# A gated state-space convolution: the order of the transforms at block ends, and one table load

## The chip, the cores and the metric

The kernel runs on one core of a Trainium2 chip. The core's engines have their own instruction streams: PE (matmuls and their weight loads), DVE (elementwise), ACT (elementwise and activations), POOL (elementwise and DMA issue) and SP (DMA issue). Each works through its stream in order and waits on semaphores for the others. The metric is the time of one execution in microseconds (us). The kernel before takes 539.49 us in the median of three runs (538.57 to 540.05). A profiled execution of it, from which all single times here come, took 540.43 us.

## The reference

For an input `u` of 2048 positions and 512 channels the reference normalizes each position and feeds two branches: a long convolution with a kernel `K` made from a state-space model, plus a skip `u * Dskip`, and a two-layer network with GELU. The result is `u + s * silu(ffn)`.

```python
xn = _layernorm(x, axis=-1)
K  = jnp.einsum("dn,dnl,dn->dl", Cc, P, dB).real      # P = exp(dt*A*l), 2048 long, per channel
Yf = rfft(pad(xn)) * rfft(pad(K))                      # length 4096
s  = irfft(Yf)[..., :L] + xn * Dskip
g  = silu(gelu(xn @ w1 + b1) @ w2 + b2)
out = x + s * g
```

All of it is in float32.

## The kernel before

The first 395 us compute the normalized input, the network and the convolution kernel; matmuls fill PE there. The change does not touch that part. Then the convolution runs in four blocks of 128 channels, b = 0 to 3. A Fourier transform of 2048 positions is split in two stages of matmuls, 64 by 32:

- `first_dft(b, u, h, parts)`, L891, is the first transform. `u` is 0 for the signal and 1 for the kernel, `h` picks 16 of 32 channel columns, and each of the two `parts`, called halves here, fills two PSUM banks. `first_out`, L899, copies them into the big tile `X`, on ACT or, where `engs` says V, on DVE.
- `second_dft(b, g)`, L913, is the second transform, for g = 0 to 7. `spectrum` (L921, ACT) copies the kernel's spectrum `uh` out of PSUM, `product` (L931, DVE) multiplies it with the signal's, and `combine` (L941 and L939, DVE) forms the real and imaginary parts `Y` out of the products of two g.
- `back_dft(b, j)`, L950, is the backward step on one `Y`, with the table `tcn`; `back_out` (L961, ACT) copies it into `Z`. `turn` (L970, DVE) transposes `Z` into `T`.
- `last_dft`, L990, is the last transform, on `T`. It fills four banks `y` at once. `last_out` multiplies them by the gate on DVE (L997) and adds the input on POOL (L998), four of each.

Two g make a slot: blocks 0 to 2 run `two_slots(b, i)` for i = 0 to 3, and in its shadow each slot runs a quarter of the first transform of block b + 1, backward steps of block b or b - 1, and in slot 2 of blocks 1 and 2 the last transform of block b - 1. Block 3 runs `slot(3, g)`, in which nothing is changed. The order of the calls is the order in each engine's stream; no scheduler moves them.

Beside these stand the loads. `side_piece` (L839, SP) fetches a `raw` piece of a later block's signal, four pieces per block; `side_turn` (L858, ACT) reorders it, a quarter at a time, into the first transform's input `in`. `kernel_half` (L874, SP) fetches half of a block's kernel, and `side_skip` (L879, POOL) adds the skip coefficients to that half before `first_dft` with u = 1 reads it. `ct_load` (L817, SP) fetches one of four pieces of the table `tcn`; backward step j of block 0 needs piece j. `tail_load` (L979, SP) fetches gate and input for `last_out`. Each of these is preceded by a one-column DVE memset (`pace`, L801), which sets the time of issue. `loads(b, g, late)` is called twice per g and looks up in a small table which load to issue there.

All banks of L891, L950 and L990 come from one helper, `bank`, which hands out four PSUM banks in turn; the second transform has four banks of its own, two per g.

## Time and profile before

| | |
|---|---|
| median of three runs | 539.49 us (538.57 to 540.05) |
| profiled execution | 540.43 us, span 538.6 us |
| PE busy | 516.0 us (96%) |
| DVE busy | 434.5 us (81%) |
| ACT busy | 388.6 us (72%) |
| POOL busy | 260.5 us (48%) |
| mean granted PE clock | 0.994 of full speed |
| block 0, from its first L913 | 395.25 to 426.95 us |
| block 1 | 426.95 to 459.93 us |
| block 2 | 459.93 to 495.73 us |

The chain that ended last is followed back from the last instruction; each of its rows is a start, a length, and the engine and line that held the end up. A row of a timeline is start, length, engine, line, operation, output and input, the count, and in brackets how long the engine stood idle before it and who released it. Queries by window give busy us and count of PE, the granted clock, the share of DMA time and GB/s.

### The profile page before, as it was taken

Reading aid. Unit: us, or ns where it says so; the run is one execution under the profiler, and the core shown is the slowest. Engines: PE = TensorE matmul, PEld = TensorE weight load, DVE = VectorE, ACT = ScalarE, POOL = GpSimd, SP = SyncE. Lnnn points to the kernel's source line nnn. Section 1 sums busy time; section 2 is a strip of 40 time slices with the busy share of each in tenths; the row PEclk is TensorE's granted clock in tenths of the full one; section 3 lists DMA queues with packets and bytes.
Section 4 is the critical chain, followed back from the end, with each engine's and each line's share of the span. In section 5 each row is a group of like instructions: output and inputs, shape, how many; then the busy total and the mean of one; then the engine's idle time right before and its main releaser. Section 6 shows DMA issues by size and latency. Waiting matters only on the chain.

```text
span 538.6 us, 16527 instructions
## 1 busy us (share of the span) xinstructions
PE 516.0 (96%) x6999; PEld 420.8 (78%) x6999; DVE 434.5 (81%) x732; ACT 388.6 (72%) x552; POOL 260.5 (48%) x384
## 2 busy tenths in 40 slices
PE   8899999999999999999999999999999799898993
PEld 8687788787877777777777777778889798878971
DVE  6998999999998689786875777896377489677896
ACT  3688896999987987896978799797365563633430
POOL 5629376756796576869726464564010004013031
PEclk9999999999999999999999999999999999999997
DMA  8937437843229992354147232952567468242562
GB/s 228 320 103 243 125 128 232 283 146 109 90 80 289 301 277 64 136 151 125 42 130 231 102 80 87 185 138 99 178 231 164 83 218 178 82 160 80 178 204 95
DMA packets 86086, 85.84 MB, mean 159 GB/s; under 512 B 41878, under 2 KB 60698, under 8 KB 84988
## 3 DMA queue, kind: packets, MB, share of 16 engines
q1 hardware_dynamic: 76944, 66.43, 41.9%
q0 software_dynamic: 8768, 17.83, 10.8%
q8 instruction: 55, 0.90, 0.7%
q10 hardware_dynamic: 300, 0.53, 0.3%
q14 instruction: 19, 0.16, 0.1%
HBM read 51.22 MB, written 33.55 MB: 157 GB/s over the span
## 4 chain that ended last, share of the span: by engine, by line
PE 80%; DVE 8%; DMA 3%; ACT 3%; POOL 3%; issue 2%; POOLq 0%; DVEq 0%; ACTq 0%
PE s L913 10%; PE z L287 9%; PE z L289 8%; PE z L288 8%; PE f L248 8%; PE f L250 8%; PE f L249 8%; PE sa L950 5%; PE kg L655 5%; PE s L891 5%; PE ph L591 2%; PE y L990 1%; DMA tcn<-in_ct_dram 1%; DMA w1s<-in_B_w_dram 1%; DVE T L970 1%
## 5 line engine op out<-in xcount | busy, mean ns | idle before, releaser
L616 POOL TENSOR_TENSOR mm<-mm,rc 128x32 f32<-128x32 f32 (+4 forms) x150 | 97.0, 647 | 11.8
L287 PE MATMUL z<-w2h,hh 128*128 128x512 f32 x224 | 95.7, 427 | 0.0
L248 PE MATMUL f<-xh,w1h 128*128 128x512 f32 x220 | 91.6, 416 | 0.2 <-DVE hl L274 0.2
L250 PE MATMUL f<-xh,w1l 128*128 128x512 f32 x220 | 87.0, 396 | 2.5 <-DVE w1l L233 1.5
L289 PE MATMUL z<-w2h,hl 128*128 128x512 f32 x224 | 87.7, 392 | 0.1
L288 PE MATMUL z<-w2l,hh 128*128 128x512 f32 x224 | 87.6, 391 | 0.0
L249 PE MATMUL f<-xl,w1h 128*128 128x512 f32 x220 | 86.8, 395 | 0.0
L913 PE MATMUL s<-X,mc 64*64 64x128 f32 x1536 | 58.3, 272 | 4.7 <-DVE X L899 4.7
L605 DVE SCALAR_TENSOR_TENSOR ra<-ra,ph 128x512 f32<-128x512 f32 x64 | 43.7, 683 | 19.4 <-ACT ra L599 18.5
L931 DVE TENSOR_TENSOR t<-s,uh 128x512 f32<-128x512 f32 x64 | 40.8, 681 | 17.7 <-ACT uh L921 17.3
L921 ACT COPY uh<-s 128x512 f32<-128x512 f32 x32 | 18.8, 586 | 47.9 <-PE s L913 26.3
L913 PEld LDWEIGHTS s<-X,mc 64*64 64x64 f32 x1536 | 45.2, 133 | 9.6 <-DVE X L899 5.3
L262 ACT ACTIVATE f<-f,b1s 128x512 f32<-128x512 f32 x56 | 37.2, 665 | 19.8 <-PE f L250 18.5
L639 DVE TENSOR_TENSOR e<-mm,ra 128x1024 f32<-128x1024 f32 x32 | 43.0, 1347 | 10.3 <-ACT ra L627 4.5
L250 PEld LDWEIGHTS f<-xh,w1l 128*128 128x128 f32 x220 | 41.3, 188 | 12.0 <-DVE w1l L233 2.0
L289 PEld LDWEIGHTS z<-w2h,hl 128*128 128x128 f32 x224 | 42.0, 188 | 10.2 <-DVE hl L274 0.6
L248 PEld LDWEIGHTS f<-xh,w1h 128*128 128x128 f32 x220 | 41.5, 189 | 10.7 <-issue 1.1
L287 PEld LDWEIGHTS z<-w2h,hh 128*128 128x128 f32 x224 | 42.4, 189 | 9.2 <-ACT hh L268 0.4
L613 POOL COPY mm<-rc 128x32 f32<-128x32 f32 x30 | 14.6, 488 | 70.6 <-DVE e L646 39.5
L288 PEld LDWEIGHTS z<-w2l,hh 128*128 128x128 f32 x224 | 42.2, 189 | 8.2
L249 PEld LDWEIGHTS f<-xl,w1h 128*128 128x128 f32 x220 | 41.3, 188 | 9.2
L274 DVE TENSOR_TENSOR hl<-f,hh 128x512 fp32r<-128x512 f32 x56 | 37.7, 681 | 10.8 <-ACT hh L268 10.8
(184 smaller groups left out, 1132.1 us busy)
## 6 DMA issues: line engine op xcount, KB each, us to landing
x<-in_A_u_dram SPq DMA_DIRECT2D x8, 512.0 KB
xs<-x SPq DMA_DIRECT2D x8, 512.0 KB
xt_h<-xh POOLq DMA_DIRECT2D x4, 1024.0 KB, 5.8
xt_l<-xl POOLq DMA_DIRECT2D x4, 1024.0 KB, 8.1
kgd<-ko SPq DMA_DIRECT2D x16, 256.0 KB
za<-zo SPq DMA_DIRECT2D x4, 1024.0 KB
xh<-xt_h POOLq DMA_DIRECT2D x4, 1024.0 KB, 6.6
xl<-xt_l POOLq DMA_DIRECT2D x4, 1024.0 KB, 9.0
```

Source lines behind the costliest of these rows:

```text
L248: PE.matmul(p, wh[:, k, :], xh[:, k, :], start=(k == 0), stop=False)
L249: PE.matmul(p, wh[:, k, :], xl[:, k, :], start=False, stop=False)
L250: PE.matmul(p, wl[:, k, :], xh[:, k, :], start=False, stop=(k == KD - 1))
L274: V.tensor_sub(hl, hf, hh)
L287: PE.matmul(z, hh[:, s], wh, start=(f0 == 0 and not rows), stop=False)
L288: PE.matmul(z, hh[:, s], wl, start=False, stop=False)
L289: PE.matmul(z, hl[:, s], wh, start=False, stop=(f0 == FA - 1))
L605: V.scalar_tensor_tensor(ra[:, 0, c], ra[:, 1, c], MAGIC, p, op0=ALU.subtract, op1=ALU.subtract)
L616: GP.tensor_mul(mv[:, :, 0:3:2, w:2 * w], mv[:, :, 0:3:2, 0:w], rc[:, 2 + 2 * i:4 + 2 * i, :].rearrange("p j c -> p c j").unsqueeze(3).to_ ...
L639: V.tensor_mul(e1, m1.unsqueeze(1).to_broadcast([P, 2, CH, N1]), ra[:, :, :, :N1])
L913: PE.matmul(p[ka * 64:(ka + 1) * 64, r, o, :, jj], w, xf[b][h, c, :, k, :], start=(c == 0), stop=(c == 1), skip_group_check=True)
L931: V.tensor_mul(t, p[:, i, :, 1].unsqueeze(1).to_broadcast([P, 2, 2, P]), uh)
```

## The change

Three things move in `two_slots`, and one in the table of `loads`.

1. At the end of a block (slot 3) both halves of the next block's first transform stand ahead of the backward step, and the combine stands behind it. Before, the second half stood behind the backward step, ahead of the next block's second transform.
2. In slot 2 of blocks 1 and 2 the last transform stands behind both second transforms, which have one half of a first transform between them. The other half goes to slot 3. The multiplications of `last_out` stand behind the combine.
3. The four quarters of `side_turn` stood two at a block's end (slot 3) and two in the next block's slot 0; now one stands in slot 3, ahead of the backward step, two in slot 0 and one in slot 1, behind that slot's first spectrum copy. `turn(b - 1, 1, 1)` goes from the end of slot 1 to the start of slot 2, behind a memset that fetches a raw piece.
4. In block 0 the third piece of `tcn` is loaded at g = 2 instead of g = 4 and the fourth at g = 4 instead of g = 6.

```diff
         if b == 0:
             plan = {(1, 0): lambda: mc_load(2), (1, 1): lambda: ct_load(1), (2, 0): lambda: mc_load(3),
-                    (4, 1): lambda: ct_load(2), (6, 1): lambda: ct_load(3)}
+                    (2, 1): lambda: ct_load(2), (4, 1): lambda: ct_load(3)}
...
+        if end:
+            turn(b - 1, 1, 1)
         second_dft(b, g)
         if end:
-            py = [bank(f"y{b - 1}_{n}").rearrange("p e m -> p (e m)") for n in range(G)]
-            last_dft(b - 1, 0, py)
-            last_dft(b - 1, 1, py)
+            first_dft(*f, (0,))
         second_dft(b, g + 1)
         spectrum(b, g)
-        if b and i == 0:
-            side_turn(b + 1, (2,))
+        if b and i < 2:
+            side_turn(b + 1, (1 + 2 * i,))
         loads(b, g, 0)
         product(b, g)
         if end:
+            first_out(*f, parts=(0,))
+            py = [bank(f"y{b - 1}_{n}").rearrange("p e m -> p (e m)") for n in range(G)]
+            last_dft(b - 1, 0, py)
+            last_dft(b - 1, 1, py)
+            spectrum(b, g + 1)
+            loads(b, g, 1)
+            product(b, g + 1)
+            loads(b, g + 1, 0)
+            combine(b, i, 1)
+            combine(b, i, 0)
             last_out(b - 1, py)
...
+        else:
+            if b and i == 3:
+                k = b + 1, 1, 0
+                first_dft(*k, (1,))
+            first_dft(*f, (0,))
+            spectrum(b, g + 1)
...
+            product(b, g + 1)
+            if b and i == 3:
+                first_out(*k, parts=(1,))
+            if i == 3:
+                first_out(*f, parts=(0,))
+                first_dft(*f, (1,))
+                first_out(*f, (A, A, V, V), (1,))
+                if b + 2 < NB:
+                    side_turn(b + 2, (0,))
+                for k in sa:
+                    back_dft(*k)
+                    back_out(*k)
+                loads(b, g + 1, 0)
+                combine(b, i, 1)
+                combine(b, i, 0)
...
         if b and i == 0:
-            side_turn(b + 1, (3,))
-        if b + 2 < NB and i == 3:
-            side_turn(b + 2, (0, 1))
+            side_turn(b + 1, (2,))
         if b and i < 2:
-            for k in (((0, 0), (0, 1)), ((1, 0), (1, 1)))[i]:
+            for k in (((0, 0), (0, 1)), ((1, 0),))[i]:
                 turn(b - 1, *k)
```

In slots 0 to 2 of block 0 and slots 0 and 1 of the others the calls of the `else` branch keep the order they had.

What this does to the streams is seen best in the order itself. The names: `s1_2_1_0_1_0` is the first transform of block 2, u = 1, h = 0, half 1, its bank 0; `s2_1_4` the second transform of block 1, g = 4; `sa1_1_0` the backward step of block 1, j = 1; `y0_0` the last transform of block 0; numbers behind them are buffer numbers.

PE in block 0, slot 3, before (the first instruction of each call):

```order
L913 MATMUL s2_0_7_5452<-X0_4893,mc_4874 64x2x64 x8
...
L891 MATMUL s1_1_1_1_0_0_5491<-fc_98,in1_1_4980 128x128
...
L950 MATMUL sa0_2_0_5507<-tcn_5040,Y_0_2_5401 128x128
...
L891 MATMUL s1_1_1_1_1_0_5530<-fc_98,in1_1_4980 128x128
...
L913 MATMUL s2_1_0_5548<-X1_5041,mc_4874 64x2x64 x8
```

and now:

```order
L913 MATMUL s2_0_7_5454<-X0_4893,mc_4874 64x2x64 x8
...
L891 MATMUL s1_1_1_1_0_0_5493<-fc_98,in1_1_4980 128x128
...
L891 MATMUL s1_1_1_1_1_0_5509<-fc_98,in1_1_4980 128x128
...
L950 MATMUL sa0_2_0_5523<-tcn_5040,Y_0_2_5403 128x128
...
L913 MATMUL s2_1_0_5547<-X1_5041,mc_4874 64x2x64 x8
```

The half whose copies the next block's second transform needs has gone ahead of the backward step.

PE in slots 2 and 3 of block 1, before:

```order
L913 MATMUL s2_1_4_5824<-X1_5041,mc_4874 64x2x64 x8
...
L990 MATMUL y0_0_5857<-T0_0_5680,gc_5044 32x512
...
L913 MATMUL s2_1_5_5893<-X1_5041,mc_4874 64x2x64 x8
...
L891 MATMUL s1_2_1_0_0_0_5942<-fc_98,in1_2_5753 128x128
...
L891 MATMUL s1_2_1_0_1_0_5965<-fc_98,in1_2_5753 128x128
...
L913 MATMUL s2_1_6_5978<-X1_5041,mc_4874 64x2x64 x8
...
L891 MATMUL s1_2_1_1_0_0_6050<-fc_98,in1_2_5753 128x128
...
L950 MATMUL sa1_1_0_6064<-tcn_5040,Y_1_1_5800 128x128
...
L891 MATMUL s1_2_1_1_1_0_6087<-fc_98,in1_2_5753 128x128
```

and now:

```order
L913 MATMUL s2_1_4_5824<-X1_5041,mc_4874 64x2x64 x8
...
L891 MATMUL s1_2_1_0_0_0_5857<-fc_98,in1_2_5753 128x128
...
L913 MATMUL s2_1_5_5867<-X1_5041,mc_4874 64x2x64 x8
...
L990 MATMUL y0_0_5910<-T0_0_5679,gc_5044 32x512
...
L913 MATMUL s2_1_6_5966<-X1_5041,mc_4874 64x2x64 x8
...
L891 MATMUL s1_2_1_0_1_0_6038<-fc_98,in1_2_5753 128x128
...
L891 MATMUL s1_2_1_1_0_0_6048<-fc_98,in1_2_5753 128x128
...
L891 MATMUL s1_2_1_1_1_0_6066<-fc_98,in1_2_5753 128x128
...
L950 MATMUL sa1_1_0_6080<-tcn_5040,Y_1_1_5800 128x128
```

The last transform went behind the second second transform, one half went to slot 3, and three halves now stand there in a row.

DVE in slots 2 and 3 of block 1, before (the products and multiplications by their first instruction):

```order
L931 TENSOR_TENSOR t0_1_4_5928<-s2_1_4_5824,uh_1_4_5926 128x4x128
...
L997 TENSOR_TENSOR gb0_5045<-y0_0_5857,gb0_5045 128x16x32
...
L931 TENSOR_TENSOR t0_1_4_5928<-s2_1_5_5893,uh_1_5_5952 128x4x128
...
L941 TENSOR_TENSOR Y_1_2_5962<-t0_1_4_5928,t1_1_4_5929 128x2x256
L939 TENSOR_TENSOR Y_1_2_5962<-t0_1_4_5928,t1_1_4_5929 128x2x256
```

and now:

```order
L931 TENSOR_TENSOR t0_1_4_5902<-s2_1_4_5824,uh_1_4_5900 128x4x128
...
L931 TENSOR_TENSOR t0_1_4_5902<-s2_1_5_5867,uh_1_5_5946 128x4x128
...
L941 TENSOR_TENSOR Y_1_2_5954<-t0_1_4_5902,t1_1_4_5903 128x2x256
L939 TENSOR_TENSOR Y_1_2_5954<-t0_1_4_5902,t1_1_4_5903 128x2x256
L997 TENSOR_TENSOR gb0_5045<-y0_0_5910,gb0_5045 128x16x32
```

The multiplications went behind the second product and the combine. POOL's own order is the same in both: four additions L998, then the skip addition L879 for the second kernel half.

## The prediction

> **What bounds the kernel now.** I read the page first, then the chain of work that ended last, then the waits of PE between 380 and 500 us, then each engine's timeline there. The change lies in the slots of blocks 0 to 2, 395 to 496 us of a 538.6 us span; nothing ahead of them is touched.

> ```profile
> PE 516.0 (96%) x6999; PEld 420.8 (78%) x6999; DVE 434.5 (81%) x732; ACT 388.6 (72%) x552; POOL 260.5 (48%) x384
> ```
> ```profile
> PE s L913 <- DVE X L899: 4.7, 3, 1.7
> ```

> PE is busy 96% of the span, so what the change can win is what PE stands idle in its slots. The second fence, of PE's waits, says that 4.7 us of it are three waits of the second transform (L913) for DVE's copies into X (L899): one at each block's end. The chain shows them, and one more loss in block 0:

> ```profile
> 413.94 7.06 DMA tcn<-in_ct_dram
> 421.13 0.68 PE sa L950 x7
> 421.81 1.25 issue
> 423.07 1.71 PE sa L950 x25
> ...
> 425.60 1.30 DVE X L899 x2
> 426.95 3.72 PE s L913 x128
> ...
> 434.44 3.65 PE s L913 x128
> ...
> 439.19 1.79 PE sa L950 x32
> ...
> 443.77 3.11 PE y L990 x64
> 446.88 1.91 PE s L913 x64
> 448.79 1.99 PE s L891 x32
> ...
> 457.38 0.69 DVE Y L941
> ...
> 458.67 1.21 DVE X L899 x2
> 459.93 3.72 PE s L913 x128
> ...
> 482.21 0.85 issue
> ...
> 495.73 3.72 PE s L913 x128
> ```
> ```profile
> 415.94 0.67 PE L913 MATMUL s<-X,mc 64*64 64x128 f32 x16
> ...
> 441.80 0.67 PE L913 MATMUL s<-X,mc 64*64 64x128 f32 x16
> ...
> 477.09 0.67 PE L913 MATMUL s<-X,mc 64*64 64x128 f32 x16
> ...
> 479.00 2.41 PE L990 MATMUL y<-T,gc 32*32 32x512 f32 x64
> ```

> The reader sees PE's units: a pair of second transforms 3.65, one alone 1.91, two halves of a first transform 1.99 (1.0 each), a backward step 1.79, a last transform 3.11. The last fence (PE's timeline) gives where slot 3 of block 0 and slots 2 of blocks 1 and 2 start. So slot 3 of block 0 takes 426.95 - 415.94 = 11.01, for 3.65 + 2 x 1.0 + 1.79 = 7.44 of work; slots 2 and 3 together take 18.13 in block 1 (to 459.93) and 18.64 in block 2 (to 495.73).

> **Part 1, block 0: the table load goes ahead of the raw pieces, both halves ahead of the backward step.** The backward step waited for the third table piece, whose DMA was issued at 413.94 behind three raw pieces on SP's queue. It now goes out one slot earlier, ahead of them, and the fourth takes its old place ahead of the last raw piece; the first raw piece still waits for the same memset. I cost the queue at nothing: the raw data's readers, ACT's reordering copies, are priced as a rival.

> ```profile
> 419.59 1.16 PE L891 MATMUL s<-fc,in 64*128 64x128 f32 x16
> ...
> 420.78 1.07 ACT L899 COPY X<-s 128x512 f32<-128x512 f32 x2 [0.43 <-PE s L891]
> ```

> Counted from the slot's start: second transforms to 3.65, both halves to 5.65. ACT's copies of the first half begin 1.19 after that half's start (420.78 - 419.59) and take 1.07: 3.65 + 1.19 + 1.07 = 5.91, when its two banks are free for the backward step, so PE waits 0.3 and ends at 5.95 + 1.79 = 7.75. DVE's two copies of the second half run 5.65 to 6.95, under the backward step: the wait of 1.27 is gone. From 11.01 to 7.75 is 3.26. In it sits the "issue" stall of 1.25, for which the profile names no cause; it may come back at the same instruction count, so the bounds are 2.0 and 3.3, and lacking any row that decides I take the middle, 2.6.

> **Part 2, blocks 1 and 2: slots 2 and 3 together.** Here one half of the first transform stands between the two second transforms, the last transform behind them, and the other half moves to slot 3. PE from the slot's start: 1.91, half to 2.9, second transform to 4.8, last transform to 7.9 (or 7.2 where it takes 2.4, as in block 2's row), then slot 3's pair and the moved half to 12.6 (11.9). But the multiplications by the gate (L997) now stand on DVE behind the second product and the combine, and POOL's four additions (L998) behind them, and behind those, on POOL in unchanged order, the skip addition L879 into the very kernel half that slot 3's next half reads.

> ```profile
> 463.76 0.58 ACT L921 COPY uh<-s 128x512 f32<-128x512 f32 x1 [0.16 <-ACT in L858]
> ...
> 464.38 1.29 DVE L931 TENSOR_TENSOR t<-s,uh 128x512 f32<-128x512 f32 x2 [0.45 <-ACT uh L921]
> ```
> ```profile
> 446.87 2.48 DVE L997 TENSOR_TENSOR gb<-y,gb 128x512 f32<-128x512 f32 x4 [0.50 <-PE y L990]
> ...
> 451.86 1.76 DVE L939 TENSOR_TENSOR Y<-t,t 128x512 f32<-128x512 f32 x1
> ...
> 481.53 2.48 DVE L997 TENSOR_TENSOR gb<-y,gb 128x512 f32<-128x512 f32 x4 [0.16 <-PE y L990]
> ```
> ```profile
> 441.76 0.23 POOL L879 TENSOR_TENSOR in<-in,dsk 128x16 f32<-128x16 f32 x1 [41.86 <-DMA in<-kgd]
> 447.64 5.42 POOL L998 TENSOR_TENSOR xb<-gb,xb 128x512 f32<-128x512 f32 x4 [5.65 <-DVE gb L997]
> 453.03 0.68 POOL L879 TENSOR_TENSOR in<-in,dsk 128x16 f32<-128x16 f32 x1
> ...
> 483.07 5.41 POOL L998 TENSOR_TENSOR xb<-gb,xb 128x512 f32<-128x512 f32 x4 [6.25 <-DVE gb L997]
> ...
> 513.86 4.97 POOL L998 TENSOR_TENSOR xb<-gb,xb 128x512 f32<-128x512 f32 x4 [24.73 <-DMA last<-in_u_rows_dram]
> ```

> The second spectrum copy starts 0.18 after its transform, 463.76 against 463.58 (459.93 + 3.65): 5.0. The product follows 0.62 later (464.38 - 463.76) and takes 1.24: 6.9. The combine, 1.29 from 457.38 to 458.67, ends at 8.15. The first multiplication starts there instead of at 5.07 (446.87 - 441.80). POOL follows 0.77 later (447.64 - 446.87): 8.9. The four additions took 5.42, 5.41 and 4.97. In block 1 they met the combine on DVE, whose second instruction took 1.76 instead of 0.69; now the combine is over before they start, and what DVE does beside them reads PSUM. I take 4.97, nearest to that: 13.9, and 0.23 for the skip addition, the row with no such neighbour: 14.1. PE's half, ready at 12.6 or 11.9, therefore waits 1.5 to 2.2 for POOL, where before the skip addition ended 3.0 into slot 3 with its half due at 3.65. Then the half to 15.1 and the next to 16.1; ACT's copies end at 14.1 + 1.19 + 1.07 = 16.4, the backward step at 18.2, and DVE's X copies lie under it. So the two slots take about 18.2: against 18.13 a loss of 0.1 in block 1, against 18.64 a gain of 0.4 in block 2, of which the 0.85 "issue" stall may take all and more (-0.5); I take 0. The bubble at the block's end is removed and a wait of the same size stands inside slot 3.

> The bounds of POOL's chain: 0.77 + 4.97 + 0.23 = 5.97 below, and 1.54 (483.07 - 481.53) + 5.42 + 0.68 = 7.64 above, 1.7 more in each block.

> [...]

> **Part 3, ACT and DVE in slots 0 and 1.** The fourth reordering copy moves into slot 1, between two spectrum copies. DVE's memset ahead of the kernel load waits for it.

> ```profile
> 462.50 1.11 ACT L858 COPY in<-raw 128x512 f32<-128x512 f32 x1
> ...
> 471.77 0.32 SPq L874 DMA_DIRECT2D in<-kgd  x1
> 476.31 0.51 POOL L879 TENSOR_TENSOR in<-in,dsk 128x16 f32<-128x16 f32 x1 [22.60 <-PE sa L950]
> ```

> Behind a slot's first spectrum copy such a copy starts 2.6 into the slot (462.50 - 459.93), so it ends near 3.7; the two products and the combine then run on DVE to 3.7 + 2 x 1.24 + 1.29 = 7.5, when the slot's last X copy falls due (7.43 of PE work): nothing on PE. The kernel half is issued at 3.9; it was landed and had its skip added 5.05 after issue (476.82 - 471.77), so at 8.9. The moved half needs it at 7.43 + 1.91 = 9.3: hidden with 0.4 to spare, and without that cover up to 1 us per block. The transpose moved behind a memset costs nothing: its reader, the last transform, starts 2.9 later than before.

> **The sum.** 2.6 - 0.1 + 0 = 2.5. The profiled execution took 540.43 (span 538.6), so it would be 537.9; the median of the runs is 539.49, 0.94 below that execution, so the forecast is 537.0.

> **Rivals.** (a) The skip addition does not hold PE: then slots 2 and 3 are PE's own, 7.9 (7.2) + 3.65 + 3 x 1.0 + 0.4 for ACT's bank + 1.8 = 16.8 (16.1), winning 1.3 and 2.5 more, with block 0 in all about 6.4: 533.1. Against it: POOL's queue is in order and 5.97 us long. (b) Slower: POOL's chain runs at its upper bound, its place is the wait of slot 3's half, and it decides from 1.25 us more per block on, where the sum is nothing. At 1.7 more, with both "issue" stalls kept (2.0 - 1.8 - 2.2), 541.5. For it: 483.07 lagged by 1.54; against: two other rows lag less and meet the combine. (c) Block 0 does not win what it should: ACT's first reordering copy now stands ahead of the backward step's output copies. It is due at 5.9, and with its 1.11 and their 1.07 must be over when the next spectrum copy falls due, 7.75 + 2.0 = 9.75 (its 0.58 end where a reordering copy starts, at 2.6): raw pieces that land over 1.7 late push the next block, and with 1.6 lost so the time is 538.6, no measurable change. (d) The new gap of 1.5 to 2.2 us lets the granted clock fall:

> ```profile
> PEclk9999999999999999999999999999999999999997
> ```
> ```profile
> 530.00:530.25 0.25, 0.22 (x16) 1.00 0.00 0
> ...
> 532.00:532.25 0.25, 0.00 (x0) 0.51 0.00 0
> ```

> At the kernel's end it fell to a half about 2.0 after the last matmul. Four us of matmuls at half speed behind each gap would cost up to 4 each: 545. Against: the stall of 1.25 at 421.81 left the page's row (each digit 13.5 us, 9 is full) at 9. [...]

> **How the numbers follow.** The forecast's mechanism 0.57, its own range 535.9 (3.3 - 0.1 + 0.4) to 538.6, (a) 0.08, (b) 0.16, (c) 0.13, (d) 0.06. A measurement of this kernel can tell about 0.3%, 1.6 us. Faster by more: 0.47 of the forecast's 0.57 and (a): 0.55. Within: the other 0.10, (c), and 0.05 of (b): 0.28. Slower: the rest of (b) and (d): 0.17. The range leaves out (a), (d) and the outer end of (b): 535.3 to 540.4.

> **What would show it.** Right: L913 no longer waits for L899 at block ends; PE's L891 waits 1.5 to 2.2 for POOL L879 in slots 3 of blocks 1 and 2; L997 starts 8.1 after slot 2's start; block 0's slot 3 takes 7.8 to 9.0. Wrong: a wait of L891 in slot 2 for the kernel load, of ACT for raw, or a clock below 1.00.

## The result, and the profile after

The changed kernel takes 539.98 us (median of 12 runs, 539.09 to 541.61) against 540.15 for the kernel before (12 runs, 538.38 to 542.53): ratio 1.000, 95% interval 0.9983 to 1.0017. That is no change where 537.0 was forecast. Of the 2.5 us that the sum promised, 0.2 arrived, with 0.9 to either side.

The profiled execution took 539.87 (span 538.0). The waits of PE in the changed kernel (total us, times, longest) show what was exchanged: the line of L913 waiting for L899 is gone, and the half of the first transform (L891) waits for POOL's skip addition (L879) in its place.

```profile
PE s L891 <- POOL in L879: 3.9, 2, 2.3
...
PE s L913 <- issue: 0.6, 1, 0.6
...
PE s L891 <- issue: 0.2, 1, 0.2
```

PE's timeline of the changed kernel (start, length, what it runs, idle time ahead of it): block 0's slots 2 and 3, then blocks 1 and 2, where slots 2 start at 439.76 and 476.64.

```profile
395.37 0.67 PE L913 MATMUL s<-X,mc 64*64 64x128 f32 x16
...
408.56 0.67 PE L913 MATMUL s<-X,mc 64*64 64x128 f32 x16
...
411.94 0.77 PE L913 MATMUL s<-X,mc 64*64 64x128 f32 x19 [0.56 <-issue]
...
416.96 0.67 PE L913 MATMUL s<-X,mc 64*64 64x128 f32 x16
...
422.37 0.72 PE L891 MATMUL s<-fc,in 64*128 64x128 f32 x9 [0.15 <-issue]
...
424.91 0.67 PE L913 MATMUL s<-X,mc 64*64 64x128 f32 x16
...
439.76 0.67 PE L913 MATMUL s<-X,mc 64*64 64x128 f32 x16
...
454.08 2.99 PE L891 MATMUL s<-fc,in 64*128 64x128 f32 x32 [2.31 <-POOL in L879]
456.85 2.70 PE L950 MATMUL sa<-tcn,Y 64*128 64x128 f32 x32
459.48 0.67 PE L913 MATMUL s<-X,mc 64*64 64x128 f32 x16
...
476.64 0.67 PE L913 MATMUL s<-X,mc 64*64 64x128 f32 x16
...
490.91 2.06 PE L891 MATMUL s<-fc,in 64*128 64x128 f32 x32 [1.61 <-POOL in L879]
492.79 2.48 PE L950 MATMUL sa<-tcn,Y 64*128 64x128 f32 x32
495.20 0.67 PE L913 MATMUL s<-X,mc 64*64 64x128 f32 x16
```

By these starts and those shown of before, slot 3 of block 0 takes 7.95 us, not 11.01, but its slot 2 takes 8.40 (416.96 - 408.56) because an "issue" stall now stands there; the whole block takes 29.54 (424.91 - 395.37) against 31.70, 2.16 less. Slots 2 and 3 take 19.72 in block 1 (459.48 - 439.76; before 18.13) and 18.56 in block 2 (before 18.64). So 2.16 - 1.59 + 0.08 = 0.65, about the difference of the two spans, 538.6 and 538.0.

The same two stretches differ by 1.1 us behind POOL's wait. From the start of the waiting half to the next block it is 459.48 - 454.08 = 5.40 in block 1 and 495.20 - 490.91 = 4.29 in block 2, for the same instructions. The table of stretches of the changed kernel says why (columns: stretch, its length, PE's busy time, the granted clock, DMA share, GB/s).

```profile
448.16:451.57 3.41, 3.41 (x109) 1.00 1.04 128
451.57:454.99 3.42, 1.11 (x20) 1.00 0.28 57
454.99:458.40 3.41, 3.41 (x38) 0.50 0.75 279
...
489.12:492.53 3.41, 1.80 (x32) 1.00 0.30 109
492.53:495.95 3.42, 3.42 (x68) 1.00 0.55 202
526.66:530.08 3.42, 2.43 (x99) 1.00 0.03 7
530.08:533.49 3.41, 0.00 (x0) 1.00 0.37 137
533.49:536.90 3.41, 0.00 (x0) 0.50 0.46 171
```

In block 1 the granted clock was 0.50 from 454.99 to 458.40, 3.41 us, and then 1.00 again. At the kernel's end it fell at 533.49, 78.50 us behind 454.99, which is 23 times 3.413. The stretches above are cut on that grid: the one ahead of a fall held 1.11 us of PE's work out of 3.42, or none; the one with block 2's wait held 1.80, and no fall came.

### The profile page after: what moved, and what is told of

Same layout as the page of the kernel before. It is cut to its first block, busy times and chain, and to the rows that moved or that the text cites. A ratio compares the mean times of both kernels' runs of the same rounds, so it can differ in the third digit from the quotient of the medians.

```text
span 538.0 us, 16528 instructions
## 1 busy us (share of the span) xinstructions
PE 517.1 (96%) x6999; PEld 422.4 (79%) x6999; DVE 428.2 (80%) x728; ACT 391.2 (73%) x556; POOL 258.1 (48%) x384
## 5 line engine op out<-in xcount | busy, mean ns | idle before, releaser
L913 PE MATMUL s<-X,mc 64*64 64x128 f32 x1536 | 58.7, 272 | 0.6 <-issue 0.6
L931 DVE TENSOR_TENSOR t<-s,uh 128x512 f32<-128x512 f32 x64 | 40.8, 683 | 18.3 <-ACT uh L921 14.9
L913 PEld LDWEIGHTS s<-X,mc 64*64 64x64 f32 x1536 | 45.4, 133 | 5.7 <-issue 1.0
L921 ACT COPY uh<-s 128x512 f32<-128x512 f32 x32 | 18.8, 587 | 40.4 <-PE s L913 23.2
```

The costliest lines, as they stand in the source:

```text
L913: PE.matmul(p[ka * 64:(ka + 1) * 64, r, o, :, jj], w, xf[b][h, c, :, k, :], start=(c == 0), stop=(c == 1), skip_group_check=True)
L931: V.tensor_mul(t, p[:, i, :, 1].unsqueeze(1).to_broadcast([P, 2, 2, P]), uh)
```

## The experiments

Theory A: the skip addition, last in POOL's queue, holds PE in blocks 1 and 2 and takes back what block 0 wins. Theory B: the clock's fall behind that wait costs the rest. Theory C: PE's "issue" stalls hide a gain that is there. Each run below has the kernel before beside it on the same chip; its medians were 540.28 (first four), 540.97 (next four), 540.82 (next three) and 539.89 (last).

**The skip addition first.** One line moves POOL's skip addition ahead of the gate's additions.

```
             combine(b, i, 0)
+            side_skip(b + 1, (1,))
             last_out(b - 1, py)
...
-        if i in (1, 2):
+        if i in (1, 2) and not end:
             side_skip(b + 1, (i - 1,))
```

> The changed kernel, with POOL's skip addition for the second kernel half (L879) issued ahead of the four additions of the last output instead of behind them. Theory (the new wait of PE for POOL, 2.31 and 1.61 us in the changed kernel's trace, and the half clock behind the longer one hold back the gain of blocks 1 and 2): PE no longer waits for POOL in slot 3, slots 2 and 3 of blocks 1 and 2 take 16.3 to 17.3 us instead of 19.7 and 18.6, the clock stays at 1.00 there, and the time is 3.5 to 5 us below the kernel before (535 to 536.5). Rival (the banks or the copies of ACT and DVE hold those slots as long): the wait goes to another engine and the time stays within 1.6 us of the kernel before.

Measured 535.14 us (534.07 to 538.00), ratio 0.9921 (0.9890 to 0.9951). It is faster than both kernels. POOL's timeline and PE's, of this kernel, in block 2:

```profile
480.10 0.23 POOL L879 TENSOR_TENSOR in<-in,dsk 128x16 f32<-128x16 f32 x1 [2.40 <-DMA in<-kgd]
485.75 4.97 POOL L998 TENSOR_TENSOR xb<-gb,xb 128x512 f32<-128x512 f32 x4 [5.42 <-DVE gb L997]
```
```profile
476.70 0.67 PE L913 MATMUL s<-X,mc 64*64 64x128 f32 x16
...
488.03 3.36 PE L891 MATMUL s<-fc,in 64*128 64x128 f32 x47
...
493.31 0.67 PE L913 MATMUL s<-X,mc 64*64 64x128 f32 x16
```

The skip addition now runs when its kernel half has landed, 5 us ahead of the additions, and PE goes from one half into the next two without a gap. Slots 2 and 3 take 493.31 - 476.70 = 16.61 in place of 18.56. In block 1, where this execution has stalls of 0.61 and 1.23 put down to "issue", they take 18.53 (459.53 - 441.00) in place of 19.72, so the 16.3 to 17.3 of the theory came in block 2 only. PE waits for POOL in neither block. Theory A holds.

**The table piece alone.** Only the order of the table pieces, on the kernel before.

```
-                    (4, 1): lambda: ct_load(2), (6, 1): lambda: ct_load(3)}
+                    (2, 1): lambda: ct_load(2), (4, 1): lambda: ct_load(3)}
```

> The kernel before, with the third and fourth table pieces alone loaded earlier. Theory: the backward step of block 0, slot 3 no longer waits for the table (0.38 us), and the stall without a cause behind it (1.25) stays on PE's stream at about the same instruction: 0 to 0.6 us won. Rival: that stall is part of the wait for the table, and 1.6 us are won.

Measured 540.07, ratio 1.000 (0.9979 to 1.0020). PE's timeline of it:

```profile
412.39 0.77 PE L913 MATMUL s<-X,mc 64*64 64x128 f32 x19 [0.56 <-issue]
...
423.69 1.71 PE L950 MATMUL sa<-tcn,Y 64*128 64x128 f32 x25 [1.02 <-issue]
...
477.63 0.67 PE L913 MATMUL s<-X,mc 64*64 64x128 f32 x16
...
495.17 0.67 PE L913 MATMUL s<-X,mc 64*64 64x128 f32 x16 [1.73 <-DVE X L899]
```

The wait of 0.38 for the table piece is gone. A stall of 0.56 has come at the very instruction where the changed kernel has one (x19 of L913), and the old one of 1.25, at x25 of the backward step, is still 1.02. So in this trace the new place of the stall came with the loads, not with PE's new order. It is not there in every execution: two traces below with the same table loads and PE's new order (six matmuls in the gap, the longer gap) list no stall in that slot. Block 2, which is as before here, has no stall in this trace, and its slots 2 and 3 take 495.17 - 477.63 = 17.54.

**Block 0's part alone.** The table piece and the two halves ahead of the backward step, in block 0 only; blocks 1 and 2 as before.

```
+        if b == 0 and i == 3:
+            first_out(*f, parts=(0,))
+            first_dft(*f, (1,))
+            first_out(*f, (A, A, V, V), (1,))
+            for k in sa:
+                back_dft(*k)
+                back_out(*k)
...
+        else:
```

> The kernel before, with the table pieces loaded earlier and both halves ahead of the backward step in block 0 alone; blocks 1 and 2 are as before. Theory: this is the gain of the change, 2.2 us in the traces (block 0 from 31.7 to 29.5 us), and nothing is given back: 1.8 to 2.6 us faster, 537.5 to 538.3. Rival (a stall moved into another place): within 1 us of the kernel before.

Measured 539.90, ratio 0.9993 (0.9973 to 1.0013): a miss for the theory, the rival's number came. The stalls in PE's timeline of it:

```profile
413.59 0.77 PE L913 MATMUL s<-X,mc 64*64 64x128 f32 x19 [1.14 <-issue]
...
424.57 0.72 PE L891 MATMUL s<-fc,in 64*128 64x128 f32 x9 [0.70 <-issue]
...
446.37 2.17 PE L990 MATMUL y<-T,gc 32*32 32x512 f32 x43 [1.08 <-issue]
```

Block 0 took 30.45 us (396.55 to 427.00), 1.25 less than before; without the 1.84 that its stalls are listed with it is 28.61, against 31.70 - 1.25 - 0.38 = 30.07 before (stall and wait for the table taken out), so by the listed times 1.46 was won by the order itself. In this execution a third stall of 1.08 in block 1 gave most of that back.

**Matmuls in the gap.** Six matmuls into the bank that the waiting half overwrites, in slot 3 of blocks 1 and 2.

```
+            for _ in range(fill):
+                PE.matmul(ps[0][:, 0, :], ident, ident, start=True, stop=True, skip_group_check=True)
...
-                first_dft(*f, (0,))
+                first_dft(*f, (0,), fill=6 if b and i == 3 else 0)
```

> The changed kernel, with six matmuls of the identity on PE ahead of the half that waits for POOL in slot 3 of blocks 1 and 2 (about 1.7 us of work whose result is overwritten). The wait for POOL's result stays as it is. Theory (the gap of 2.3 us lets the granted clock fall to a half for about 3.4 us, which costs 1.6 us): the clock stays at 1.00 in blocks 1 and 2, slots 2 and 3 of block 1 take 18.1 to 18.5 us instead of 19.7, and the time is 1 to 2 us below the changed kernel. Rival (the slower matmuls behind the gap are slow for another reason, such as the DMA traffic of the stores that starts there): no difference to the changed kernel, or the fill's own length is lost.

Measured 540.71, ratio 1.0011 (0.9990 to 1.0032): a miss in time, where the rival's "no difference" came. The clock did stay at 1.00 in blocks 1 and 2, and block 1's wait was filled; but stalls of 0.22 and 0.68 fell into the same two slots, and they took 19.84. This run does not tell what the fall of the clock is worth.

**A longer gap.** A copy on POOL between the additions and the skip addition.

```
             last_out(b - 1, py)
+            w = gx[b - 1][1][:, :, :N1]
+            GP.tensor_copy(w, w)
```

> The changed kernel with one copy of 128x512 in place (about 1.08 us on POOL, as POOL's rows of L858 show) between the gate's additions and the skip addition in slot 2 of blocks 1 and 2; the output is the same. Theory (the clock is judged in windows of 3.41 us, and a gap that fills more than half of one halves the clock for the next): PE's gaps grow from 2.3 and 1.6 us to about 3.4 and 2.7, so the clock falls in block 1 always and in block 2 mostly, each fall costing about 1.6; with 2.2 of longer waits and about one fall more per execution than in the changed kernel: 543.5 to 544.5, and the mean granted clock 0.988 to 0.990. Rival (only a gap over a whole window lets the clock fall; the one fall seen was chance): longer waits alone, 542 to 542.5, clock 0.992.

Measured 541.53, ratio 1.0023 (1.0001 to 1.0046), mean granted clock 0.9899 over its runs. The copy took 0.57 us, not 1.08, so POOL's chain grew by half of what was meant, and the time lies below both theories' numbers. In the traced execution the clock stayed at 1.00 in blocks 1 and 2: PE came late itself, by stalls put down to "issue", and waited 0.89 and 2.16 for POOL. What speaks for theory B is the mean clock of the runs: 5 of 10 had 0.988 or less, against 2 of 12 of the changed kernel, measured apart from these, and none of the 25 of the kernel before on the same chip.

**The raw pieces from whole rows.** The kernel with the skip addition first; the raw pieces of blocks 2 and 3 arrive as 8 KB a partition, not as pieces of 128 B.

```
+        if b > 1:
+            whole = xs.rearrange("(k p n) (m d) -> k p (n m) d", k=NB * G, p=N1, d=DB)
+            SY.dma_start(t[g * N1:(g + 1) * N1], whole[b * G + g])
+        else:
```

> The kernel with the skip addition first, in which the raw pieces of blocks 2 and 3 are read from whole rows of the same tensor (8 KB a partition in place of pieces of 128 B): other data, so the output is another; sizes, queue and waits are the same. Theory (PE's 'issue' stalls are instruction packets that queue behind the small data packets): the stalls around 412 and 424 us, 0.5 and 1.0 in the kernel it is made from, go to 0.2 or less, and those of block 1 too; 1 to 2 us faster than that kernel, 533 to 534. Rival (the stalls come from elsewhere): the same stalls at the same instructions, 535 to 535.5.

Measured 535.21 (534.32 to 536.03), ratio 0.9900 (0.9873 to 0.9927): a miss for the theory's 533 to 534, in the rival's range. Against its own kernel before it is some 0.6 us better than the kernel it was made from, which is within the noise; the spread of its runs is smaller. The stalls did shrink, from 3.3 listed in that kernel's trace (the slowest of its six runs) to 0.5, and the traces suggest what they wait for. The DMA view of half a microsecond of the kernel before, ahead of its stall at 421.81, and of this kernel at the same place (packets, MB, time that they took as a share of 16 engines; the last section sets q8's packets against PE's instructions):

```profile
q1 hardware_dynamic: 303, 0.04, 142.3%
q8 instruction: 1, 0.02, 21.2%
```
```profile
q8 instruction: 1, 0.02, 14.8%
q1 hardware_dynamic: 6, 0.02, 11.0%
```

A packet on q8 (16 KB each: 0.90 MB in 55 packets by the page) took 1.70 us (21.2% of 0.5 us times 16) beside 303 small data packets, and 1.18 beside 6. In this kernel's trace no stall is listed in block 0, and one of 0.51 stands in block 1. The 14 traces together list 33 such stalls of PE between 396 and 520 us, and each ends 1.3 to 1.9 us behind the end of a packet on q8 (1.55 and 1.37 in the kernel before, 1.44 and 1.50 in the changed one). With their fixed places in PE's stream (last section) I take them for waits for instructions, an inference from these times: no view names what a stall waits for. A packet slowed by small ones is not behind every stall: ahead of the 0.85 at 482.21 in the kernel before, it took 1.07 beside one small packet.

**Blocks 1 and 2 alone, with the old and the new place of the skip addition.** Block 0 and its table pieces as before, but with one reordering copy at block 0's end, not two.

```
-            if i == 3:
+            if b and i == 3:
                 first_out(*f, parts=(0,))
                 first_dft(*f, (1,))
```

> Blocks 1 and 2 as in the changed kernel, block 0 and the order of its table pieces as in the kernel before. Theory (in the changed kernel block 0 wins 1.5 to 2.2 and blocks 1 and 2 lose it to POOL's chain and the clock): 0.5 to 2 slower than the kernel before, 540.8 to 542.2, clock near 0.992. Rival (blocks 1 and 2 are even, as predicted, and block 0 wins nothing): the same as the kernel before, 540 to 540.5.

> The same with the skip addition ahead of the gate's additions, block 0 as before. Theory (POOL's chain takes 1.9 to 2.3 a block, block 0's part is worth 1.5 to 2): 536.5 to 537.2, about 3.3 below the kernel before and 1.5 to 2 above the kernel with both. Rival (block 0's part is worth nothing): 535 to 535.5.

The second has the line of the first experiment besides. Measured 541.88, ratio 1.0010 (0.9987 to 1.0033), and 537.07, ratio 0.9943 (0.9919 to 0.9966); both lie where their theories had them, though the first by itself cannot be told from the kernel before. The place of one POOL instruction is worth 541.88 - 537.07 = 4.8 us here by the medians (3.6 by the two ratios), as it was with block 0's part (540.0 to 535.1). Block 0's part is worth the difference of two gains, 5.1 with it and 3.9 without it: 1.2, with 2 to either side by the two intervals, so that this difference alone does not show that it wins.

**Both kernels without the small packets, and the gap filled again.** The whole-row loads of above in the kernel before, in the changed kernel, and in the changed kernel with six and with three matmuls in the gap.

> The kernel before, with the raw pieces of blocks 2 and 3 read from whole rows (other data, so the output is another). Theory (the small packets hold up PE's instruction packets): the stalls of 1.25 and 0.85 go to 0.3 or less each, 1.2 to 2 faster than the kernel before, and the times of its runs lie closer together. Rival: the same time and the same stalls.

> The changed kernel with the same loads (other data, so the output is another). Compared with the kernel before with these loads, with next to no 'issue' stalls in either. Theory: block 0 wins 1.4 for the two halves ahead and 0.4 for the table piece, blocks 1 and 2 lose 0.1 and 0.8 to POOL's chain and the clock takes 1.1 on average (a fall of about 1.6 in two runs of three): 0 to 0.4 slower, within what can be told; mean granted clock about 0.992 against 0.994. Rival (the forecast's sum was right and the stalls hid it): 1.5 or more faster than the kernel before with these loads.

> The changed kernel with the same loads and six more matmuls in PE's gap in blocks 1 and 2 (other data, so the output is another; the six are overwritten by the half behind them). Theory (falls of the clock cost about 1.1 on average): 0.8 to 1.3 faster than the changed kernel with these loads, mean granted clock 0.994 or more, no fall in the trace. Rival (the falls cost nothing on average, as the earlier run with six matmuls had it): within 0.4.

> The changed kernel with whole-row loads (other data, so the output is another) and three matmuls in PE's gap in place of six, about 0.8 us. Theory A (the six were too long in the executions whose gap was short, and so took back what the clock gave): the gaps left are 0.7 to 1.5, the clock stays, 538.3 to 538.9, below the same kernel without the matmuls. Theory B (extra instructions in PE's stream cost, whatever they fill): 540 or more, with a clock of 0.994.

| kernel with whole-row loads | median us (range) | ratio to the kernel before | mean clock |
|---|---|---|---|
| before | 538.98 (537.35 to 540.82) | 0.9961 (0.9943 to 0.9978) | 0.9939 |
| changed | 539.26 (537.75 to 541.50) | 0.9980 (0.9961 to 1.0000) | 0.9931 |
| changed, six matmuls | 540.44 (538.92 to 542.51) | 1.0002 (0.9983 to 1.0020) | 0.9946 |
| changed, three matmuls | 539.62 (539.01 to 541.42) | 0.9993 (0.9975 to 1.0012) | 0.9948 |

The small packets cost the kernel before 1.8 us, with 0.9 to either side; its stall of 1.25 is gone, that of 0.85 is still 0.57. Without them the changed kernel is still no faster than it (+0.3 by the medians, +1.0 by the ratios, with 1.4 to either side), about as its theory had it: the stalls did not hide a gain of 1.5 or more, and theory C falls as the explanation of the miss. PE's timeline of the changed kernel with these loads (its lines from the loads on are numbered four higher) has the fall of the clock again, now in block 2:

```profile
455.68 2.06 PE L895 MATMUL s<-fc,in 64*128 64x128 f32 x32 [1.49 <-POOL in L883]
...
459.98 0.67 PE L917 MATMUL s<-X,mc 64*64 64x128 f32 x16
...
491.39 3.62 PE L895 MATMUL s<-fc,in 64*128 64x128 f32 x32 [2.03 <-POOL in L883]
...
496.79 0.67 PE L917 MATMUL s<-X,mc 64*64 64x128 f32 x16
```

From the waiting half to the next block: 4.30 without a fall, 5.40 with one, the same 1.10 as above. The 12 runs of this kernel part into two groups: five with a mean clock of 0.990 or 0.991 (mean 541.0 us), six of 0.995 or 0.996 (538.5); one lies between, at 0.992. The kernel before with these loads has three of 11 runs at 0.990 or 0.991 too, so falls in it are not ruled out, though no trace shows one. But a long wait both can have a fall behind it and is long itself, so that the whole 2.5 is the clock's is not shown. And the two kernels with matmuls in the gap, whose mean clock was 0.994 or more in every run, were not faster: six missed both their theory and its rival by being 1.2 slower, and three, on another chip, came out between their two theories. Their traces show no new wait; the six matmuls left block 1's two slots at 18.62, and block 2's at 18.93 against 18.56 of the changed kernel. Theory B is shown for the executions traced, 1.1 us a fall; its average over the runs stays open, and so does what the matmuls themselves cost.

## Why the prediction was wrong

The wait that comes and the wait that goes were right; the steps that failed are terms of the sum. Block 0 was put at 2.6 and gave 1.3 to 1.8; blocks 1 and 2 were put at -0.1 and 0 and gave -0.4 and -1.0; the clock was put at nothing and took 1.1 in the profiled execution. That 539.98 lies inside the stated range of 535.3 to 540.4 is luck: the mechanism's own range ended at 538.6, and the rest was held open for (b) and (c), which did not come.

**What bounds the kernel.** Right: the wait of L913 for L899 at the block ends went in all three blocks.

**Part 1, block 0.** The mechanism was right, and the term of 2.6 too large. Slot 3 took 7.95 for a forecast of 7.75. But the stall of 1.25, counted half as a gain, ended 1.55 behind the end of a packet on q8, by the reading above a wait for instructions, and with the earlier table load a stall stood in slot 2 instead. It is no property of the order: the stalls behind 400 us added up to 0.7, 1.6, 2.1 and 3.3 us in the profiles of the changed kernel, the table alone, before, and block 0 alone. What the order wins is 1.46, what the table piece wins 0.38, together 1.8 where 2.6 was counted. Two traces with whole-row loads that list no stall in block 0 give less, 29.96 before (426.05 - 396.09) and 28.69 changed, with three matmuls (423.90 - 395.21): 1.3. In the runs' times it is 0.4 (alone, 1.1 to either side) to 1.2 (2 to either side).

**Part 2, blocks 1 and 2.** This step failed most, though its chain came out nearly to the number. POOL's timeline of the changed kernel:

```profile
448.88 4.96 POOL L998 TENSOR_TENSOR xb<-gb,xb 128x512 f32<-128x512 f32 x4 [8.14 <-DMA raw<-xs]
453.80 0.22 POOL L879 TENSOR_TENSOR in<-in,dsk 128x16 f32<-128x16 f32 x1
...
485.70 4.97 POOL L998 TENSOR_TENSOR xb<-gb,xb 128x512 f32<-128x512 f32 x4 [7.66 <-DVE gb L997]
490.62 0.23 POOL L879 TENSOR_TENSOR in<-in,dsk 128x16 f32<-128x16 f32 x1
```

The additions start 9.1 after slot 2 (forecast 8.9) and take 4.96 and 4.97 (4.97), and the waiting half starts at 14.3 (14.1). The waits are 2.31 and 1.61 (1.5 to 2.2). DVE's multiplications (L997) and products (L931) ran beside the additions, from 448.12 to 452.98 in block 1; that the additions would take no longer for it was the author's estimate. The skip addition took 0.22 and 0.23 (0.23). From there three sizes were wrong. The rest of the slot took 4.29 where 4.1 was counted, so the two slots need 18.56, not 18.2. In block 2 this was set against 18.64, which holds a stall listed with 0.85. Between the bounds of 0.4 and -0.5 that this gave, the prediction took 0; the stall belonged on neither side. Without one the old order needs 17.54 there, as the trace with the table piece alone shows: the stall had made it 1.1 longer, more than its listed time. So the order itself loses 1.0 in block 2 and 0.4 in block 1, where the sum had 0 and -0.1. And in block 1 the clock fell, 1.1 more, where the sum had nothing.

**Part 3.** Right: the kernel half landed in time, and no half waited in slot 2.

**The sum as the traces have it.** Block 0 +1.3 to +1.8, block 1 -0.4, block 2 -1.0: -0.1 to 0.4 are left, and one fall of the clock takes 1.1. A fall of 3.41 us at half lowers an execution's mean clock by 0.003, and the changed kernel's mean over its runs was 0.9920 against 0.9934 to 0.9946 of the kernel before on the four chips of the experiments: half a fall more each or somewhat over, an estimate of 0.5 to 0.9. That leaves -1.0 to -0.1, which the measured gain of 0.2, with 0.9 to either side, does not contradict; the last term is the one that the runs did not show by itself.

**The rivals.** (a) did not come, since the skip addition did hold PE; where it does not, in the first experiment, 4.8 more is won than by the change (3.9 was priced). (b) did not come: the additions stayed at 4.97. (c) did not come either: no reordering copy waited for raw data. (d) was given 0.06 and happened, in block 1. That the clock would stay at 1.00 was the author's estimate, which the run did not bear out. The argument against it, that a stall of 1.25 had left the page's row at 9, said nothing about a gap of 2.3. Nor does that row show a fall of 3.41 us: the changed kernel's has no digit below 9 around 455 us either:

```profile
PEclk9999999999999999999999999999999999999998
```

The price was 1.1, not "up to 4". Half speed lasted 3.41 us, and part of that time is likely one in which PE waits for ACT's copies anyway: without a fall the stretch takes 4.29 for 3.8 of work.

## What to carry to other kernels

A bubble that is removed by moving work can come back as a wait on the engine whose queue the moved work lengthened: here 4.7 us of waits for DVE's copies went, and 3.9 of waits for POOL came. Before accepting such a wait, look down that queue for the one short instruction that PE needs, and let it go ahead: here 0.23 us of POOL's work, moved ahead of 5 us of additions, was worth more than the whole rearrangement. Keep "issue" stalls out of both sides of a comparison before you compare slots, best by an execution that has none there: a stall listed with 0.85 had made its slots 1.1 longer.

## What the runs showed of the hardware

```profile
458.63:462.04 3.41, 1.57 (x56) 1.00 0.00 2
462.04:465.45 3.41, 3.41 (x102) 1.00 0.02 5
```
```profile
529.18:532.59 3.41, 1.62 (x80) 1.00 0.03 7
532.59:536.00 3.41, 0.00 (x0) 0.50 0.41 154
```

With 1.57 us of work no fall came in the first (the table alone), with 1.62 one came in the second, so these traces set no sharp bound, only one near half. A gap can therefore cost more than itself or not, by where it lies on the grid: a fall came behind the waits of 2.31 (changed kernel) and 2.03 (whole-row loads), none behind the 2.16 of the longer gap, whose stretch held 1.73 us of work out of 3.41. The kernel before, with a stretch of 0.49, is near the bound too.

**Instruction packets.** PE's stalls fall on fixed instructions of its stream (x19 of L913, x25 of L950 and x9 of L891 recur in several kernels, with 253 matmuls and as many weight loads, 506, between x19 and x9 in block 0 of the changed kernel, about two packets: its page counts 6999 matmuls, 6999 weight loads and 55 packets on q8, 254.5 instructions a packet if q8 carries these alone). Behind 396 us their listed times add up to 0.7 to 3.3 us in the nine traces with data pieces of 128 B, and to 0.5 to 0.6 in the five with whole rows. So they make a good part of the difference between single executions of kernels with the small pieces.
